# Moving the state sums and the next scores into the run of 64x64 products of a visit

## The chip, the cores and the metric

The kernel runs on one core of a Trainium2 chip. The metric is the device time of one execution, in microseconds; before the change it is 638.41 us, the median of three runs (637.95 to 638.81). The profile was taken in a further execution, whose span on the core is 636.0 us. All times below are read from that profile, in microseconds from the start of the span.

## The reference, cut to what matters

```python
# attention: 4 batches, 8 heads, 768 tokens, 64 dims
for t in range(S):
    state = gamma * state + einsum('bhd,bhe->bhde', k[:, :, t], v[:, :, t])
    y[:, :, t] = scale * einsum('bhd,bhde->bhe', q[:, :, t], state)
x = y.transpose(0, 2, 1, 3).reshape(3072, 512)
# feed-forward: 512 -> 2048 -> 512, leaky relu between
h = x @ w_in
out = maximum(0.01 * h, h) @ w_out
```

## The kernel before, in words

**Tiling.** The tokens are cut into six chunks (`c`, 0 to 5) of 128 tokens per batch. Within a chunk the recurrence is written as masked scores times values plus reads of the state; between chunks the state is a sum of keys times values. The feed-forward part works through four units (`u`, 0 to 3) of 512 hidden columns for each chunk. Its matrix products are made by a seven-product scheme at two levels, so that every unit is a chain of products on the tensor engine with additions on the vector engine and copies on the scalar engine around them. All data are FP32, and each product leaves two weight loads and two matmul records in the trace.

**Two parts.** Chunks 0 and 1 go through the feed-forward units in the first part, in which the weights are also prepared and kept in DRAM. The second part begins near 230 us. It goes through chunks 2 to 5, sixteen units (`n`), with weights that are streamed back from DRAM for each unit: `wa` for the first group of the inner products, `wb` for the second. The order of everything is written out by hand; there is no scheduler. Each engine goes through its own queue in program order, and waits on semaphores where it needs another's work.

**One unit of the second part** (main loop, L1281 to L1323) is, on the tensor engine: the inner products of the next unit with `wa` (L1184, 128x128 tiles with 128 columns), then seven output products of this unit (`output`, made by `seven`, L662, 128x128 tiles with 256 columns), with the inner products of the next unit with `wb` between the fourth and the fifth of them. The output products go in the order M1, M5, M6, M2, M7, M3, M4 into four PSUM banks named A to D, which are banks 5, 4, 7 and 6. M1 in A is copied to B by the scalar engine (L755), because M6 is added to it there. The inner products work in banks 0 to 3.

**Attention in the second part.** While chunk `c` is in units 0 and 1, the attention of chunk `c + 1` is computed, two batches at a time (a *pair*: batches 0 and 1 in unit 0, batches 2 and 3 in unit 1). There are two excursions for a pair, both with 64x64 tiles of the array, four of which work side by side:
- `scores_of_pair` (L356): the scores of the pair (L369, q against k) and the sums of keys times values for each half of the chunk (L380), 64 records each. The vector engine then masks the scores (L387, tiles `am`) and adds the sums to the state in two steps: the state in the middle of the chunk, `mid`, and the new state. It uses banks 0 to 3. It is called for the *following* pair, after the third output product. For chunk 5 the second half of the sums isn't needed, and the new state neither.
- `joint_visit` (L412): values against masked scores (L444) and reads of the old state and of `mid` with q (L427), 128 records, into banks 1, 2, 0 and 7. The vector engine multiplies the four results with the decay table `gq` and puts them into the chunk's `x` (L466, here called the *takens*). It comes right after the inner products with `wa`.

[...] So a product that follows such another waits for a mark: a GpSimd memset of one column (`rows_free`, L408), which itself waits for the last product of the earlier group. `crossed` tells which half of the rows a value product uses.

`next_gq` (L95) multiplies the decay table by one chunk's decay; it is four instructions on the scalar engine (L100), once for each new chunk, before its first pair is scored. `of_pair` loads the values (kind 1) or keys (kind 0) of a pair, `decay_v` scales the values on GpSimd, `ahead` loads q and k of a batch. `load_unit` asks for the streamed weights. All these loads are issued by one queue in program order. `outer(n + 1, 0)` (L1210) is two additions on the vector engine that follow the inner products with `wa`.

Of the kernel before, what the change touches and what calls it, by code (L numbers as in the profile page):

```python
# [22 lines left out]
def kernel(  # L23
# [329 lines left out]
    mid_of = {}  # L353
    quads = [(m, i, 2 * m + i) for m in range(HP // 2) for i in range(2)]

    def scores_of_pair(c, b, banks=None, mid=None):  # L356

        if b == 0 and c > JOINED:
            next_gq()
        banks = banks or bank  # L360
        at = [banks[j].rearrange("p (b m i t) -> p b m i t", b=2, m=HP // 2, i=2)
              for j in range(2)]
        sums = [banks[2 + h].rearrange("p (b a d) -> p b a d", b=2, a=HP) for h in range(2)]
        for n in range(2):
            x = heads[c, b + n][0]
            for m, i, a in quads:
                for h in range(2):
                    for j in range(2):
                        nc.tensor.matmul(at[j][ts(h, 64), n, m, i],  # L369
                                         lhsT=x[ts(j, 64), 1, a, ts(h, 64)],  # L370
                                         rhs=x[ts(j, 64), 0, a, ts(h, 64)],
                                         start=(n == 0 and a == 0), stop=True,
                                         skip_group_check=True)
        last = c == NC - 1
        for n in range(2):
            key, val = keys.pop((c, b + n)), vals[c, b + n]
            for a in range(HP):
                for j in range(2):
                    for h in range(1 if last else 2):
                        nc.tensor.matmul(sums[h][ts(j, 64), n, a], lhsT=key[ts(h, 64), 2 * a + j],  # L380
                                         rhs=val[ts(h, 64), 2 * a + j],
                                         start=(n == 0 and a == 0), stop=True,
                                         skip_group_check=True)
        weights = scores[c, b] = []
        for j in range(2):
            am = work.tile([128, 2, HP // 2, 2, C // 2], FP32, tag=f"am{j}", name=f"am{j}_{c}_{b}")
            nc.vector.tensor_tensor(  # L387
                out=am.rearrange("p b m i t -> p (b m i) t"),
                in0=at[j].rearrange("p b m i t -> p (b m i) t"),
                in1=mask[:, 0].unsqueeze(1).to_broadcast([128, 2 * HP, C // 2]), op=ALU.mult)  # L390
            weights.append(am)
        p = b // 2
        old = state_of[p]
        free_again[p] = [old]
        if mid is None:
            mid = halves_of_states.pop(0)
            free_again[p].append(mid)
        plus(mid, old, sums[0])
        if not last:
            state_of[p] = halves_of_states.pop(0)  # L400
            plus(state_of[p], mid, sums[1])
        mid_of[p] = old, mid
        if following(c, b) is not None and c > JOINED:
            of_pair(*following(c, b), 0)

    def rows_free(mm):

# [1 line left out]
        tc.add_manual_dep(done, mm.ins.name, IN_ORDER, reason="rows of the array")  # L409
        return done  # L410

    def joint_visit(c, b, banks=None):  # L412

        later = following(c, b) if c > JOINED else None
        banks = banks or [[bank[k] for k in at] for at in ((1, 2), (0, 7))]
        at = [[ps.rearrange("p (a t) -> p a t", t=C) for ps in of_one] for of_one in banks]
        by_half = mid_of.pop(b // 2)
        weights = scores.pop((c, b))

        def read(n, after=None):  # L420
            x = heads[c, b + n][0]
            for h in range(2):
                for m in range(HP // 2):
                    for j in range(2):
                        for i in range(2):
                            a = 2 * m + i
                            mm = nc.tensor.matmul(at[n][j][ts(i, 64), m, ts(h, 64)],  # L427
                                                  lhsT=by_half[h][ts(j, 64), n, a],
                                                  rhs=x[ts(j, 64), 0, a, ts(h, 64)],
                                                  start=(n == 0 and h == 0 and m == 0), stop=False,  # L430
                                                  skip_group_check=True)
                            if after is not None:
                                tc.add_manual_dep(mm.ins, after.name, IN_ORDER,
                                                  reason="rows of the array")
                                after = None
            return mm

        def value(n, crossed, after=None):
            val = vals[c, b + n]
            for m in range(HP // 2):  # L440
                for i in range(2):
                    for j in range(2):
                        h, a = j ^ crossed, 2 * m + i
                        mm = nc.tensor.matmul(at[n][j][ts(i, 64), m, ts(h, 64)],  # L444
                                              lhsT=val[ts(h, 64), 2 * a + j],
                                              rhs=weights[j][ts(h, 64), n, m, i],
                                              start=(n == 1 and crossed == 1 and m == 0),
                                              stop=True, skip_group_check=True)
                        if after is not None:
                            tc.add_manual_dep(mm.ins, after.name, IN_ORDER,  # L450
                                              reason="rows of the array")
                            after = None
            return mm

        done1 = rows_free(value(1, 1))
        read(0)
        done0 = rows_free(value(0, 0))
        read(1, done1)
        value(1, 0)
        value(0, 1, done0)  # L460
        for n in (1, 0):
            for j in (1, 0):
                ps = at[n][j]
                th, o = divmod((b + n) * C, N)
                blocks = xs[c][0].rearrange("p (kh th) k n -> p kh th k n", th=2)[:, :, th]
                nc.vector.tensor_tensor(out=blocks[:, j, :, ds(o, C)], in0=ps[:, 0 : HP // 2],  # L466
                                        in1=gq[:, j], op=ALU.mult)
        halves_of_states.extend(free_again.pop(b // 2))
        for n in range(2):
            heads.pop((c, b + n))  # L470
        if later is not None:
            of_pair(*later, 1)
            for n in range(2):
                decay_v(later[0], later[1] + n)

    def pair_of_banks(name):

# [2 lines left out]

    def early_scores(c, b, place):
        def do():
            banks = [pair_of_banks(f"{name}_{c}_{b}") for name in ("ap", "sp")]
            scores_of_pair(c, b, banks[0] + banks[1], place())
        return do

    def early_visit(c, b):
# [150 lines left out]

    PIECES = ((0, 0, N), (1, 0, N // 2), (1, N // 2, N))

    def seven(tiles, name, takes, takes_piece=None, order=ORDER, room=None):

        banks = {}
# [9 lines left out]
        for m, bank, sa, sb in (which[i] for i in order):  # L653
# [4 lines left out]
            for to, (i, a, z) in places:  # L658
                for n, (w, x, t) in enumerate(tiles):
                    rhs = x[:, sb] if sb < 4 else t[:, sb - 4]  # L660
                    for k in range(2):
                        nc.tensor.matmul(  # L662
                            to, lhsT=block(w, sa)[:, k, ts(i, 128)], rhs=rhs[:, k, a:z],
                            start=(first and (i == 0 or split) and n == 0 and k == 0),
                            stop=(n == len(tiles) - 1 and k == 1), skip_group_check=True)
# [385 lines left out]
    def at_of(n):  # L1051
        return 2 + n // NU, n % NU

    def load_unit(n, group):

        if n >= N2:
            return
        u = at_of(n)[1]
        if group == 0:
            wa = streamed[0]  # L1060
            nc.sync.dma_start(out=wa[:, :, 0:1], in_=kept[u][:, :, 0:1])
            nc.sync.dma_start(out=wa[:, :, 1:4], in_=kept[u][:, :, 3:6])
        else:
            wb = streamed[1]
# [194 lines left out]
    last = output(1, os[1], [parts[1]], False, True, room=room, order=FUSED)  # L1259
    products(last, 4)  # L1260
    halves_of_states.append(work.tile([128, 2, HP, D], FP32, tag="m5", name="half_states"))
    scores_of_pair(3, 0)
    for b in range(2):
        ahead(3, 2 + b)
    products(last, 1)
# [15 lines left out]
    for n in range(N2):  # L1281
# [9 lines left out]
        if n + 1 < N2:  # L1291
# [3 lines left out]
            while held:  # L1295
                held.pop()()
            products(begun, 7)
            outer(n + 1, 0)
        if visiting and u == 0:
            xs[c + 1] = new_x(c + 1)  # L1300
        if visiting:
            joint_visit(c + 1, 2 * u)
        steps = output(c, os[c], [gs.pop(n)], u == 0, u == NU - 1, room=room if more else last_room,
                       order=FUSED if more else LAST, held=held if more else None)
        products(steps, 3)
        if c + 1 < NC and u < 2 and following(c + 1, 2 * u):
            scores_of_pair(*following(c + 1, 2 * u))
        if visiting:
            load_unit(n + 2, 0)
        products(steps, 1)  # L1310
        if c + 1 < NC and u == 1:
            differences(*xs[c + 1])
        if c + 1 < NC and u == 2:
# [102 lines left out]
```

## Time and profile before

| what | value |
|---|---|
| time, median of 3 | 638.41 us |
| span of the profiled execution | 636.0 us |
| DMA, whole span | 113.42 MB, 178 GB/s |
| visits in the second part, first start | 255.69, 283.57, 357.10, 384.57, 458.29, 485.75 us |
| score runs in the second part, first start | 230.66, 263.50, 290.97, 364.50, 392.17, 465.69 us |
| granted clock of the tensor engine | 1.0 |

How to read it: "busy" of the tensor engine counts a matmul from its start to a modelled end, and matmuls overlap. An engine can therefore be busy without a gap and still work slower than it could. The distance from the start of one group to the start of the next is the better measure of what a group costs. In the timeline a line gives the start, the duration, the engine, the line of the code, the tiles of the array in use, the shape and how many records were merged; a bracket at its end gives the idle time before it and what ended it.

### The profile page before, as it was taken

To read this page: it belongs to the slowest core of one execution; us is meant where nothing else is said; L and a number is where in the kernel's file an instruction comes from. 1 tells how busy PE (TensorE), PEld (TensorE's weight loads), DVE (VectorE), ACT (ScalarE), POOL (GpSimd) and SP (SyncE) were. 2 spreads that over 40 slices of the span, in tenths; PEclk is the share of its full clock that TensorE was granted. 3 is DMA by queue.
4 is the path that set the end of the run, shared out by engine and by line. 5 is a ranking of instruction groups with operands and counts; after the bars stand their busy time and mean duration, and the time that the engine had idled before them with its cause. 6 is when DMAs were issued, how large, how long until landed. Compare 5 with 4: busy or idle time off the path is not lost.

```text
span 636.0 us, 14285 instructions
## 1 busy us (share of the span) xinstructions
PE 628.8 (99%) x6086; PEld 568.8 (89%) x6086; DVE 464.1 (73%) x760; ACT 268.9 (42%) x515; POOL 23.3 (4%) x45
## 2 busy tenths in 40 slices
PE   8999999999999999999999999999999999999997
PEld 5888888888888889899999999999999999999996
DVE  5679769889979986576785666877737768636655
ACT  4876556347343124242352442423433423534421
POOL 2000000000011010101000101000010000000000
PEclk9999999999999999999999999999999999999999
DMA  8941426556863998376735392864455236444201
GB/s 331 404 131 38 128 67 220 148 174 194 283 250 110 351 333 280 103 238 193 259 88 184 120 295 79 268 195 140 137 169 185 87 123 197 154 162 158 87 1 68
DMA packets 87537, 113.42 MB, mean 178 GB/s; under 512 B 3241, under 2 KB 71721, under 8 KB 87473
## 3 DMA queue, kind: packets, MB, share of 16 engines
q1 hardware_dynamic: 87168, 111.88, 53.2%
q8 instruction: 48, 0.79, 0.5%
q10 hardware_dynamic: 304, 0.62, 0.3%
q14 instruction: 17, 0.13, 0.1%
HBM read 93.35 MB, written 19.14 MB: 177 GB/s over the span
## 4 chain that ended last, share of the span: by engine, by line
PE 95%; DVE 2%; ACT 1%; DMA 1%; issue 0%; DVEq 0%; ACTq 0%
PE bank L662 32%; PE bank L1184 27%; PE C_h L662 4%; PE B_o L662 4%; PE A_h L662 4%; PE C_o L662 4%; PE A_o L662 4%; PE B_h L662 4%; PE D_h L662 2%; PE D_o L662 2%; PE d L683 2%; PE bank L369 1%; PE bank L444 1%; PE bank L427 1%; PE bank L380 1%; DMA t<-decay_dram 1%
## 5 line engine op out<-in xcount | busy, mean ns | idle before, releaser
L606 DVE TENSOR_TENSOR made<-made,bank 128x512 f32<-128x512 f32 (+1 forms) x96 | 56.4, 618 | 55.9 <-PE bank L1184 51.5
L606 DVE TENSOR_TENSOR o<-o,bank 128x512 f32<-128x512 f32 (+2 forms) x91 | 58.5, 661 | 51.8 <-PE bank L662 31.2
L662 PE MATMUL bank<-g,w 128*128 128x256 f32 x384 | 89.9, 382 | 0.0
L662 PEld LDWEIGHTS bank<-g,w 128*128 128x128 f32 x384 | 70.7, 190 | 9.2
L1184 PEld LDWEIGHTS bank<-x,wb 128*128 128x128 f32 x672 | 77.6, 192 | 0.8
L1184 PE MATMUL bank<-x,wb 128*128 128x128 f32 x672 | 77.6, 275 | 0.0
L1184 PE MATMUL bank<-x,wa 128*128 128x128 f32 x512 | 67.7, 275 | 0.0
L662 PE MATMUL bank<-gd,w 128*128 128x256 f32 x288 | 66.1, 379 | 0.0
L1184 PEld LDWEIGHTS bank<-x,wa 128*128 128x128 f32 x512 | 63.5, 192 | 1.1 <-ACT made L1194 0.2
L662 PEld LDWEIGHTS bank<-gd,w 128*128 128x128 f32 x288 | 54.7, 190 | 7.4
L1184 PE MATMUL bank<-t,wa 128*128 128x128 f32 x384 | 53.3, 275 | 0.0
L1226 ACT ACTIVATE g<-g 128x512 f32<-128x512 f32 x64 | 39.3, 631 | 30.8 <-DVE g L606 30.8
L1184 PEld LDWEIGHTS bank<-t,wa 128*128 128x128 f32 x384 | 48.0, 192 | 0.0
L1188 ACT COPY bank<-bank 128x512 f32<-128x512 f32 (+1 forms) x32 | 16.7, 520 | 67.8 <-PE bank L1184 67.5
L606 DVE TENSOR_TENSOR g<-made 128x512 f32<-128x512 f32 x64 | 42.7, 688 | 1.2
L755 ACT COPY bank<-bank 128x512 f32<-128x512 f32 x17 | 9.7, 570 | 71.2 <-PE bank L662 71.1
L609 DVE TENSOR_TENSOR gd<-g,gd 128x512 f32<-128x512 f32 x48 | 33.2, 692 | 5.4 <-ACT g L1226 0.5
L776 ACT COPY bank<-bank 128x512 f32<-128x512 f32 x16 | 9.1, 570 | 46.4 <-PE bank L662 46.4
L662 PE MATMUL bank<-g,last 128*128 128x256 f32 x120 | 28.3, 380 | 0.0
L662 PE MATMUL bank<-gd,last 128*128 128x256 f32 (+1 forms) x124 | 27.5, 373 | 0.0
L662 PE MATMUL A_h<-x,w 128*128 128x256 f32 x112 | 26.6, 380 | 0.0
L662 PEld LDWEIGHTS bank<-gd,last 128*128 128x128 f32 x124 | 22.8, 190 | 3.2 <-DVE gd L609 0.3
(223 smaller groups left out, 1030.1 us busy)
## 6 DMA issues: line engine op xcount, KB each, us to landing
wa<-kept SPq DMA_DIRECT2D x16, 1344.0 KB, 7.2
raw<-in_weights_dram SPq DMA_DIRECT2D x31, 512.0 KB, 4.4
wb<-kept SPq DMA_DIRECT2D x16, 896.0 KB, 5.7
wa<-kept SPq DMA_DIRECT2D x16, 448.0 KB, 4.4
wb<-kept SPq DMA_DIRECT2D x16, 448.0 KB, 6.3
out_dram<-o SPq DMA_DIRECT2D x23, 256.0 KB, 3.1
kept<-w SPq DMA_DIRECT2D x12, 448.0 KB, 6.0
qk<-in_qk_dram SPq DMA_DIRECT2D x10, 512.0 KB, 8.0
```

The source lines that it names most:

```text
L369: nc.tensor.matmul(at[j][ts(h, 64), n, m, i], lhsT=x[ts(j, 64), 1, a, ts(h, 64)], rhs=x[ts(j, 64), 0, a, ts(h, 64)], start=(n == 0 and a = ...
L380: nc.tensor.matmul(sums[h][ts(j, 64), n, a], lhsT=key[ts(h, 64), 2 * a + j], rhs=val[ts(h, 64), 2 * a + j], start=(n == 0 and a == 0), sto ...
L427: mm = nc.tensor.matmul(at[n][j][ts(i, 64), m, ts(h, 64)], lhsT=by_half[h][ts(j, 64), n, a], rhs=x[ts(j, 64), 0, a, ts(h, 64)], start=(n = ...
L606: nc.vector.tensor_tensor(out=out, in0=a, in1=b, op=ALU.add)
L609: nc.vector.tensor_tensor(out=out, in0=a, in1=b, op=ALU.subtract)
L662: nc.tensor.matmul(to, lhsT=block(w, sa)[:, k, ts(i, 128)], rhs=rhs[:, k, a:z], start=(first and (i == 0 or split) and n == 0 and k == 0), ...
L683: nc.tensor.matmul(banks[r][:, i, :], lhsT=block(2 * u, r + 2 * kh)[:, k, ts(i, 128)], rhs=x[:, 2 * kh + th, k, :], start=(step == 0 and i ...
L755: nc.scalar.copy(out=bank_of("B"), in_=ps)
L776: nc.scalar.copy(out=bank_of("D"), in_=ps)
L1184: nc.tensor.matmul(ps[q][:, i], lhsT=w[:, j, i], rhs=part_of(moving[i], s), start=(i == 0 and m in ("M1", "M5", "M4")), stop=True, skip_gr ...
L1188: nc.scalar.copy(out=ps[3], in_=ps[0])
L1226: nc.scalar.activation(g[:, i], g[:, i], AF.Prelu, alpha=0.01)
```

## The change

The two excursions of a unit become one. `scores_of_pair` is split into its parts (`scores_of`, `sums_of_states`, `masked_pair`, `new_states`), `joint_visit` into `of_visit` (which offers `read`, `value` and `taken`) and `visited`. A new `long_visit` takes the place of the visit and the score run in the main loop. It makes, in one run of 64x64 products: the crossed values, the sums of this pair's own states (into banks 5 and 4), the uncrossed values, the reads of the old state, the scores of the following pair (into banks 6 and 3), and the reads of the state in the middle. The sums so stand between the two kinds of values, which had to wait for each other's rows. A pair's state is now updated in its own visit; before, that was done with its scores, one visit earlier. The scores of chunk 3, pair 0, which have no visit ahead of them, are made alone.

Two things move with it. The additions of `outer(n + 1, 0)` come behind the visit's work on the vector engine instead of ahead of it (`behind`), and `next_gq` comes right behind them. The loads of the next weights `wa`, and then of the values and keys of the following pair, are asked for after the first output product; the weights' load carries a dependence on that product's last matmul, so that it doesn't run beside the visit. Before, the weights were asked for after the score run, the values right after the visit, and the keys of the pair after next after the score run.

The purpose is to have fewer stretches of 64x64 products between the large ones, and work between products that must wait for each other.

```diff
+    def long_visit(c, b, behind):
+        later = following(c, b)
+        read, value, taken = of_visit(c, b, [[bank[k] for k in at] for at in ((1, 2), (0, 7))])
+        done = [rows_free(value(n, 1)) for n in (1, 0)]
+        sums = sums_of_states(c, b, (bank[5], bank[4]))
+        new_states(c, b, sums)
+        for n in (1, 0):
+            value(n, 0, done[1 - n])
+        for n in (1, 0):
+            read(n, (0,))
+        if later is not None:
+            at = scores_of(*later, (bank[6], bank[3]))
+        for n in (1, 0):
+            read(n, (1,))
+        places = [(1, 1), (1, 0), (0, 0), (0, 1)]
+        if later is not None:
+            masked_pair(*later, 0, at)
+            taken(*places.pop(0))
+            masked_pair(*later, 1, at)
+        for place in places:
+            taken(*place)
+        visited(c, b)
+        behind()
+        if later is None:
+            return
+        if later[1] == 0:
+            next_gq()
+
+    def next_pair(c, b):
+        for kind in (1, 0):
+            of_pair(c, b, kind)
+        for n in range(2):
+            decay_v(c, b + n)
...
-    def load_unit(n, group):
+    def load_unit(n, group, behind=None):
...
-            nc.sync.dma_start(out=wa[:, :, 0:1], in_=kept[u][:, :, 0:1])
+            load = nc.sync.dma_start(out=wa[:, :, 0:1], in_=kept[u][:, :, 0:1])
+            if behind is not None:
+                tc.add_manual_dep(load.ins, behind.ins.name, IN_ORDER, reason="not beside the visit")
...
-    scores_of_pair(3, 0)
+    at = scores_of(3, 0, bank[0:2])
+    next_gq()
+    for j in range(2):
+        masked_pair(3, 0, j, at)
...
             products(begun, 7)
-            outer(n + 1, 0)
         if visiting and u == 0:
             xs[c + 1] = new_x(c + 1)
         if visiting:
-            joint_visit(c + 1, 2 * u)
+            long_visit(c + 1, 2 * u, lambda: outer(n + 1, 0))
+        elif more:
+            outer(n + 1, 0)
         steps = output(c, os[c], [gs.pop(n)], u == 0, u == NU - 1, room=room if more else last_room,
                        order=FUSED if more else LAST, held=held if more else None)
+        products(steps, 1)
+        if visiting:
+            load_unit(n + 2, 0, behind=newest[0])
+            if following(c + 1, 2 * u):
+                next_pair(*following(c + 1, 2 * u))
         products(steps, 3)
-        if c + 1 < NC and u < 2 and following(c + 1, 2 * u):
-            scores_of_pair(*following(c + 1, 2 * u))
-        if visiting:
-            load_unit(n + 2, 0)
-        products(steps, 1)
```

## The prediction, made before the changed kernel was run

> **What bounds the kernel now.** I read the busy times, then the chain of waits, then the tensor engine's waits in the second part (230 to 500 us), then its timeline around a visit. The first three say one thing: the chain is the tensor engine.
>
> ```profile
> PE 628.8 (99%) x6086; PEld 568.8 (89%) x6086; DVE 464.1 (73%) x760; ACT 268.9 (42%) x515; POOL 23.3 (4%) x45
> PE 95%; DVE 2%; ACT 1%; DMA 1%; issue 0%; DVEq 0%; ACTq 0%
> ```
>
> The tensor engine is busy 628.8 of 636.0 us. Among its waits between 230 and 500 us, where all that the change moves lies, there is one line:
>
> ```profile
> PE bank L427 <- DVE made L606: 0.2, 1, 0.2
> ```
>
> So taking a wait away can bring hardly anything. What is left is time in which the engine counts as busy and advances slowly, and that is seen only in the distance between starts. The timeline of the tensor engine at the visit of chunk 4, pair 0, and the run of scores and sums that follows it (start, duration, group):
>
> ```profile
> 356.34 0.83 PE L1184 MATMUL bank<-t,wa 128*128 128x128 f32 x6
> 357.10 0.46 PE L444 MATMUL bank<-am,v 64*64 64x64 f32 x16
> 357.38 0.41 PE L427 MATMUL bank<-qk,half_states 64*64 64x64 f32 x16
> ...
> 358.55 0.65 PE L444 MATMUL bank<-am,v 64*64 64x64 f32 x32
> 359.12 1.99 PE L662 MATMUL bank<-g,w 128*128 128x256 f32 x8
> 360.96 3.62 PE L662 MATMUL bank<-gd,w 128*128 128x256 f32 x16
> 364.50 1.16 PE L369 MATMUL bank<-o 64*64 64x64 f32 x64
> 365.48 1.11 PE L380 MATMUL bank<-v,k 64*64 64x64 f32 x64
> 366.53 1.99 PE L662 MATMUL bank<-g,w 128*128 128x256 f32 x8
> 368.36 4.85 PE L1184 MATMUL bank<-x,wb 128*128 128x128 f32 x42
> ```
>
> A product leaves two records. Steady steps: 80 records of 64x64 from 357.38 to 358.55, 14.6 ns each; 16 of 128x256 from 373.05 to 376.50 elsewhere in this timeline, 216 ns; 26 of 128x128 from 328.62 to 331.52, 111.5 ns. Against these the visit, 128 records, has three surcharges. The six records ahead of it last 357.10 - 356.34 = 0.76 instead of 0.67 (+0.09); the visit lasts 359.12 - 357.10 = 2.02 instead of 1.87 (+0.15, most of it in its first and last group); the eight behind it last 1.84 instead of 1.73 (+0.11). Together 0.35 us. The score run: 3.54 instead of 3.45, 2.03 instead of 1.87, 1.83 instead of 1.73, again 0.35. **An excursion into 64x64 costs about 0.35 us, however long it is.** The second part has twelve: six visits, six score runs.
>
> [...] 0.35 us at each pair of changes, and no extra step where values turn into reads at 357.38. [...] The page's instruction queue shows 48 packets for 0.79 MB, so 16 KB each[...]
>
> **The change, part by part.**
>
> Merging. The scores of the following pair and this pair's own sums move into the visit. Excursions fall from twelve to seven: six long ones, and the scores of chunk 3, pair 0, alone. The number of products is the same, and the four quarters of the array are used as before. Where chunk 5 has half the sums, 32 records take 1.03 us (393.15 to 394.18) because only two quarters work; this moves over unchanged. Saving 5 x 0.35 = 1.75 us.
>
> Order inside the run. With T its start: crossed values to T+0.52, sums to T+1.45, uncrossed values to T+1.92, old-state reads to T+2.39, next scores to T+3.32, middle-state reads to T+3.79, end E = T+3.89. Four dependences are new or moved.
> (1) The uncrossed values wait for the GpSimd marks. Marks come 0.6 to 1.1 us after the first product of their group (357.10 to 357.72; 385.32 to 386.24); now 0.93 us of sums stand between, so nothing is waited for. In the visit at 384.57 this wait is on the path today:
>
> ```profile
> 386.02 0.84 PE L444 MATMUL bank<-am,v 64*64 64x64 f32 x32
> 386.24 0.10 POOL L408 MEMSET between<- 128x1 f32 x1 [0.96 <-PE bank L444]
> 386.79 1.99 PE L662 MATMUL bank<-g,w 128*128 128x256 f32 x8
> ```
>
> The group lasts 0.77 instead of the 0.57 of the visit above: 0.20 us that go away.
> (2) The reads with the middle state wait for an addition of 0.68 us, which waits for the sums (T+1.45 and 0.23 of drain, as 365.48 to 365.71 shows before the masks) and for the vector engine, which is on the inner products' three additions until T+1.4 (356.38 + 2.11 = 358.49). Ready by T+2.4, asked for at T+3.32; even behind the second addition, T+3.1, it is early. Cost 0. Only the last visit, without scores, asks at T+2.4: 0 to 0.1.
> (3) The scores use banks 6 and 3. Bank 3 is freed by those three additions at T+1.4, asked for at T+2.39. Cost 0.
> (4) Behind the run the vector engine does mask, taken, mask, three takens (0.61 a mask from 1.29 for two, 0.33 a taken from 1.41 for four): T+3.55 to T+6.2, then two additions of the outer sums, hidden behind some 7 us of output products. The output's second product needs bank 7, free at T+4.6, asked for at E+1.84 = T+5.73. Cost 0.
>
> The one new wait on the path. After the second pair's visits of chunks 3 and 4 the scaling of the decay table (four ScalarE instructions) is now queued ahead of the copy from the first output bank to the second, on which the output's third product waits. Today the copy comes first:
>
> ```profile
> 387.40 1.41 DVE L466 TENSOR_TENSOR x<-bank,dec 128x256 f32<-128x256 f32 x4
> 388.82 0.57 ACT L755 COPY bank<-bank 128x512 f32<-128x512 f32 x1 [5.34 <-PE bank L662]
> 389.30 1.28 ACT L100 ACTIVATE dec<-dec 128x128 f32<-128x128 f32 x4
> ```
>
> The scaling waits for the takens that read the table. Third taken done at T+5.43+0.42 = T+5.85, scaling to about T+7.1 (1.28, the last overlapping), copy 0.57, third product at T+7.7. It could start at E+1.84+1.73 = T+7.46. Loss 0.24 each, 0.48 in two places; between 0 and 0.45 each, if the vector engine's steps are 0.2 faster or slower when masks and takens alternate.
>
> Start of the second part. The first score run lasts 232.82 - 230.66 = 2.16 us, 0.13 more than the others; without its sums I take the 0.13 as saved. The visit at 255.69 lasts 2.43, 0.41 too long, mostly because bank 1 is freed late (256.33). That addition follows the inner products, not what moves, so it stays.
>
> Loads. The weights for the next unit are asked for about E+2 instead of after the score run (367.08, 8 us after the visit's end), the values and keys behind them. DMA idles there and moves 300 to 400 GB/s from 366 to 381. Everything comes earlier except the value load, which has 20 us. The q and k of the following chunk, asked for at 374.3 and landing 8.2 to 9.6 us later, are now wanted at T+2.4 = 386.9 instead of 392.2; they had landed by 384.6. Cost 0 with 2.3 us in hand.
>
> Sum: -1.75 - 0.20 - 0.13 + 0.48 = -1.60, so 638.41 - 1.60 = **636.8 us**.
>
> **Rivals.**
> *Everything hides* (635.7): the scaling costs nothing, and the vector engine, free of two additions at the start, clears the waits of 0.31 and 0.36 us ahead of and in the visit at 255.69. -1.75 - 0.33 - 0.67 = -2.75. For it: the vector engine is slack. Against: those waits hang on products just before.
> *The surcharge comes back as waits* (638.0): the vector or scalar engine becomes the bound behind the run. If the third product waits 0.45 in two places and a freed bank or the middle state costs 0.1 in six visits, and the 0.33 is not found, it is -1.75 + 0.90 + 0.60 = -0.25, so 638.2; with half of those, about 637.6; I take 638.0. For it: all of the vector engine's visit work is now asked for at once. Against: the 7 us of output behind it.
> *A load comes late* (640.0, slower): the scores inside the run need q and k earlier. If they land 1.6 us late in the two visits that cross a chunk, that is +3.2 - 1.6 = +1.6. An instruction fetch that can't keep up with 512 instructions in 3.8 us would look alike. Against: 2.3 us in hand, an idle DMA[...].
>
> **How the numbers follow.** Forecast 0.55, everything hides 0.13, surcharge returns 0.20, late load 0.12. The bound of 0.2% is 1.28 us: faster means below 637.13, and the forecast with its unknowns (0 to 0.9 for the scaling) lies there four times in five. Faster 0.55 x 0.82 + 0.13 and a little of the third, 0.60; slower 0.11; same 0.29. The range runs from the second case to the upper end of the third: 635.8 to 638.4.
>
> **What would show it.** Right: one run of 256 records of about 3.9 us at each visit, no 64x64 group between output products, and surcharges of about 0.35 per run. The scaling ahead of the copy, and a third output product starting about 0.2 us late, in two visits. Wrong: a tensor-engine wait on the middle state, bank 3, or q and k; or surcharges that grow with the run's length, which would mean that they are no price of the change of mode.

## Result: 642.08 us, 0.6% slower

| | before | after |
|---|---|---|
| time, median of 4 runs | 638.18 us (637.93 to 638.81) | 642.08 us (641.45 to 642.45) |
| span of the profiled execution | 636.0 us | 640.1 us |

The ratio is 1.0059, with an interval of [1.0041, 1.0076]. A later comparison (experiment 9) gave 641.11 against 637.73, a ratio of 1.0055 [1.0041, 1.0068]. The forecast of 636.8 us was wrong in its sign.

The top of the page after the change, in the same two lines as shown of before: the busy times and the shares of the chain of waits.

```profile
PE 629.4 (98%) x6086; PEld 569.7 (89%) x6086; DVE 464.2 (73%) x760; ACT 268.9 (42%) x515; POOL 23.2 (4%) x45
PE 93%; DMA 2%; ACT 2%; DVE 2%; issue 1%; DVEq 0%
```

The busy times are those of before, the number of products is unchanged, and the granted clock is 1.0 again. New in the chain is "issue" with 1%, where it had 0%. The tensor engine's waits in the second part (from 230 us on; columns: total us, number, longest) say where it comes from:

```profile
PE bank L364 <- issue: 2.1, 2, 1.4
PE bank L433 <- issue: 1.6, 2, 1.3
PE bank L1244 <- DMA wa<-kept: 0.9, 1, 0.9
PE bank L451 <- DVE made L662: 0.2, 1, 0.2
```

Before there was one line, of 0.2 us (the last one here is a wait of 0.18 in the first visit that the kernel before has as well). L364 is the scores, L433 the reads, L451 the values: the four waits that end with "issue" lie inside the new run, and no other engine and no load ended them. In what follows v1 to v6 are the six visits of the second part in order. Here are, in the timeline, the runs of v2 (chunk 3, second pair) and of v3 (chunk 4, first pair), and the pauses in those of v4 and v5 (start, duration, group, idle time before it). v3 is the visit whose timeline the prediction shows of before.

```profile
283.20 0.69 PE L451 MATMUL bank<-am,v 64*64 64x64 f32 x32
...
285.59 1.11 PE L364 MATMUL bank<-qk 64*64 64x64 f32 x64
286.52 0.53 PE L433 MATMUL bank<-o,states 64*64 64x64 f32 x22
288.36 0.39 PE L433 MATMUL bank<-o,states 64*64 64x64 f32 x10 [1.31 <-issue]
288.68 1.99 PE L720 MATMUL bank<-g,w 128*128 128x256 f32 x8
...
360.35 0.28 PE L364 MATMUL bank<-o 64*64 64x64 f32 x5
361.99 1.09 PE L364 MATMUL bank<-o 64*64 64x64 f32 x58 [1.36 <-issue]
363.53 1.99 PE L720 MATMUL bank<-g,w 128*128 128x256 f32 x8
...
389.28 0.52 PE L433 MATMUL bank<-o,states 64*64 64x64 f32 x20 [0.27 <-issue]
...
464.87 0.34 PE L364 MATMUL bank<-o 64*64 64x64 f32 x8 [0.70 <-issue]
```

The run of v2 goes as planned, 14.6 ns a record, for 246 records; then it stops in the middle of a group of reads of which 22 have already gone out, and goes on 1.3 us later. In v3 it stops after 165 records, five records into the scores. A wait for data would be expected at the first record of a group. The bracket understates the loss, since idle time is counted from a modelled end: the whole run of v2 takes 5.48 us instead of 256 x 14.6 ns = 3.74 and the 0.15 of a visit before, so the pause cost 1.59.

**Where the 4.2 us went.** The distances between the starts of the visits place it. The first score run begins at 230.66 before and 230.57 after, so nothing came from the first part.

| stretch | before | after | difference | forecast | worked out from the trace after |
|---|---|---|---|---|---|
| first scores to v1 | 25.03 | 24.81 | -0.22 | | sums moved out -1.07, wait for `wa` +0.87 |
| v1 to v2 | 27.88 | 27.82 | -0.06 | -0.35 | excursion -0.35, slower run in v1 +0.30 |
| v2 to v3 | 73.53 | 74.76 | +1.23 | -0.11 | excursion -0.35, pause +1.59 |
| v3 to v4 | 27.47 | 28.79 | +1.32 | -0.35 | excursion -0.35, pause +1.68 |
| v4 to v5 | 73.72 | 74.05 | +0.33 | -0.31 | excursion -0.35, mark -0.20, pause +0.55, third product +0.32 |
| v5 to v6 | 27.46 | 28.04 | +0.58 | -0.35 | excursion -0.35, pause +0.92 |
| v6 to end | 150.25 | 151.26 | +1.01 | | sums moved in +1.00 |
| first scores to end | 405.34 | 409.53 | +4.19 | -1.60 | +4.21 |

The forecast for the first and last stretch together was -0.13. The pauses, 4.74 us in v2 to v5, are more than the whole loss. v1 has the same kind of loss in small: 0.19 us of its 0.30 is one step after its 146th record, in the middle of a group.

**What the pauses are.** If a run stops in the middle of a group and nothing is awaited, the instructions themselves may be missing. Three readings point to it. First, the DMA view of the stretch from 284 to 292 us (40 slices of 0.2 us, busy tenths and GB/s) shows the pause with nearly idle DMA engines, and two packets of the instruction queue around it:

```profile
DMA  0000000040000000000000000002000000000000
GB/s 0 0 0 0 0 0 0 0 82 0 0 0 0 0 0 0 0 0 0 0 0 0 0 0 0 0 0 82 0 0 0 0 0 0 0 0 0 0 0 0
...
q8 instruction: 2, 0.03, 1.8%
```

One packet begins at 285.7; the engine stops at 287.05 and goes on at 288.36, 2.7 us after that packet began, and the next packet begins at 289.5, 1.1 us after the engine has gone on. The other pauses have the same order: in v3 to v5 the engine goes on 2.9, 2.4 and 2.7 us after a packet began, and the next one begins 1.0 to 1.1 us later.

Second, the page shows 48 packets of the instruction queue (`q8 instruction`) for 0.79 MB, 16 KB each. The tensor engine has 6086 matmul records, 127 to a packet, and in experiment 2 six packets come with 768 records, 128 each. So I take a packet to hold a block of 128 records (an estimate from these counts), or 256 instructions, since the page counts a weight load beside each matmul record (x6086 both); the 6086 records make 47.5 such blocks. Between the four pauses the trace has 637, 382 and 765 records; 5, 3 and 6 blocks are 640, 384 and 768 (the two or three records less are not accounted for).

Third, all four pauses come at the second block's edge in a run, if the edges lie 128 records apart (at 118 and 246 in v2, 37 and 165 in v3, 9 and 137 in v4, 56 and 184 in v5). The runs of 128 records before the change cross one edge each, or none, and had no pause.

### The profile page after: what moved, and what is told of

It is laid out like the page before. It is cut to its first block, busy times and chain, and to the rows that moved or that the text cites. A ratio compares the mean times of both kernels' runs of the same rounds, so it can differ in the third digit from the quotient of the medians.

```text
span 640.1 us, 14280 instructions
## 1 busy us (share of the span) xinstructions
PE 629.4 (98%) x6086; PEld 569.7 (89%) x6086; DVE 464.2 (73%) x760; ACT 268.9 (42%) x515; POOL 23.2 (4%) x45
## 4 chain that ended last, share of the span: by engine, by line
PE 93%; DMA 2%; ACT 2%; DVE 2%; issue 1%; DVEq 0%
PE bank L720 31%; PE bank L1244 26%; PE C_h L720 4%; PE B_o L720 4%; PE A_h L720 4%; PE C_o L720 4%; PE A_o L720 4%; PE B_h L720 4%; PE D_o L720 2%; PE D_h L720 2%; PE d L741 2%; DMA wa<-kept 1%; PE bank L451 1%; PE bank L364 1%; PE bank L433 1%
```

## Experiments

The fetch theory is that a dense run uses instructions faster than they come: 128 records in 1.87 us, where the next block takes some 3.5 us (an estimate from v2: these 1.87 and the 1.59 lost there). Its rivals are that some product or operand inside the run is slow, that the loads or the vector engine's later work disturb it, and that the loss is the price of a longer run in itself. In the expectations FETCH stands for the first, and WAIT for a semaphore or a change of the kind of product as the cause; pairs are named there by their first batch, so that v2 is "chunk 3, pair 2"; "the mixed version" is the kernel of experiment 6, and "the plain split" that of experiment 5.

**1. The same program, shifted by 26 records.** If block edges cause the pauses, products added far ahead must move them by just so many records. Ten idle products at the start of the kernel become 36 shorter ones; these are not FP32 and leave one record each (in the changed kernel the ten, and one more behind them, leave 11).

```diff
+    def small_ones(count, cols):
...
-    keep_busy(10)
+    small_ones(36, 128)
```

> The changed kernel with 26 more weight-load and matmul pairs (52 instructions) ahead of everything on the tensor engine: the ten idle products of 512 columns at the start become 36 of 128 columns. Nothing else moves. In the changed kernel the run of products pauses after record 246 of the visit of chunk 3, pair 2 (1.31 us), after record 165 of chunk 4, pair 0 (1.36 us), after record 137 of chunk 4, pair 2 (0.27 us). Theory FETCH [...]: every pause comes 26 records earlier, after 220 and 139; the third visit, whose block edge falls out of the run's start, pauses instead near record 239 and for about 1.3 us, while the pause after 139 shrinks to about 0.3 us[...]. Time 641 to 643. Theory WAIT (the pauses belong to a semaphore or to a change from one kind of products to another): the pauses stay after records 246, 165 and 137, with their lengths.

Measured: 644.10 us against 637.66, ratio 1.0087 [1.0061, 1.0113]. That is above the 641 to 643 expected, but the 2.2 us by which the profile's span is longer lie ahead of the second part (its first scores start at 232.88). There the granted clock is 0.5 from 13.7 to 17.1 us (0.997 in the mean of the execution), where the changed kernel has 1.0; the one run of the four with a mean clock of 0.999 took 641.4 us, the others, at 0.994 to 0.997, 644 and more. From the first scores to the end it takes 409.42 us, where the changed kernel takes 409.53. The timeline of the runs of v2 and v4:

```profile
288.91 1.10 PE L364 MATMUL bank<-qk 64*64 64x64 f32 x60
290.88 0.27 PE L364 MATMUL bank<-qk 64*64 64x64 f32 x2 [0.87 <-issue]
...
392.00 0.41 PE L433 MATMUL bank<-o,half_states 64*64 64x64 f32 x15
393.44 0.47 PE L433 MATMUL bank<-o,half_states 64*64 64x64 f32 x17 [1.02 <-issue]
```

In v2 the pause comes after 160 + 60 = 220 records, where it came after 246: moved by exactly 26, and now between two scores. In v4 the edge of 137 moved to 111, and the pause came at the one after it, 239. In v5 it moved from 184 to 158, and 0.44 us are left. The pause in v3, whose edges moved to 11 and 139, is gone, and v1 got one of 1.36 us after 248 and one of 0.34 after 120, the only one at a run's first edge (by the same count the edge before it lies eight records ahead of the run). No product is slow by nature; what counts is where in the instruction stream the run lies. Shifting the program only moves the loss from run to run.

**2. A much longer run.** 384 products of 64x64 on constants, with results that nothing reads, are added between two large stretches near 408 us: 768 records with no operand to wait for.

```diff
+    def long_run():
+        for _ in range(6):
+            for m in range(16):
+                for i in range(2):
+                    for j in range(2):
+                        nc.tensor.matmul(bank[2 * j][ts(i, 64), 0:64],
+                                         lhsT=mask[ts(j, 64), 0], rhs=mask[ts(j, 64), 0],
+                                         start=True, stop=True, skip_group_check=True)
...
+        if n == 6:
+            long_run()
```

> The changed kernel with 384 more 64x64 products (768 records, 1536 instructions) of constant operands into two free banks, in one run ahead of the inner products of the seventh unit, near 431 us; nothing waits for their results. At 14.6 ns a record they need 11.2 us. FETCH [...]: after the first 128 to 256 records a pause about every 128 records, one block each 3.5 us, 17 to 20 us for the run. [...] WAIT: no pause either, since nothing in the run waits.

Measured: 662.45 us, in one run. The timeline of the tensor engine, and the DMA view of 407 to 429 us (busy tenths in slices of 0.55 us):

```profile
407.74 2.67 PE L1348 MATMUL bank<-mask 64*64 64x64 f32 x167
413.31 5.55 PE L1348 MATMUL bank<-mask 64*64 64x64 f32 x256 [2.90 <-issue]
420.49 2.09 PE L1348 MATMUL bank<-mask 64*64 64x64 f32 x128 [1.64 <-issue]
423.95 2.09 PE L1348 MATMUL bank<-mask 64*64 64x64 f32 x128 [1.36 <-issue]
427.40 1.55 PE L1348 MATMUL bank<-mask 64*64 64x64 f32 x89 [1.36 <-issue]
```

```profile
DMA  9999999100000100000100000010000010000001
```

This isolates the cause. With nothing to wait for, the run settles at 128 records every 3.46 us (420.49 to 423.95, 423.95 to 427.40), 27 ns a record instead of 14.6. The DMA engines do nothing in these stretches but carry one block every 3.5 us (30 GB/s in one slice of six or seven, 0 in the others): what limits is the time until a block comes, not their bandwidth. The same view counts `q8 instruction: 6`, six packets for the 768 records. The first pause, after 167 records, is longer, 2.90 us. Until about 411 us the DMA engines are full of data, and the packet it waits for begins only at 410.8. The 256 records behind it last 5.55 us for a second reason: from 413.3 to 416.4 the granted clock is 0.5 (0.997 in the mean of the execution), and a record takes 26.7 ns. From 416.4 on it is 1.0 again, so also in the blocks on which the 3.46 us rest. In all the run lasts 21.2 us; 17 to 20 were expected.

**3. Loads asked for beside the run.** The change asks for the weights only behind the run's first output product. This kernel asks at its start.

```diff
         if visiting:
+            load_unit(n + 2, 0)
             long_visit(c + 1, 2 * u, lambda: outer(n + 1, 0))
...
-            load_unit(n + 2, 0, behind=newest[0])
```

> The changed kernel with the streamed weights asked for at the start of the run instead of behind the first output product: 1.8 MB are then moved beside the run. FETCH: the blocks of instructions come over the same DMA engines; in the long run of constant operands a block that was asked for while data were moved held the engine up for 2.90 us instead of 1.36. So the pauses get 1 to 2 us longer in the five long visits that have one, and shift to no other record: 646 to 652 us. WAIT: nothing in the run uses these weights, so the pauses stay as they are, and the time stays at 642.

Measured: 656.55 us in one run, more than any theory had it. The run of v2 in the timeline, to be read against the one of the changed kernel above:

```profile
287.12 0.53 PE L433 MATMUL bank<-o,states 64*64 64x64 f32 x22
292.26 0.39 PE L433 MATMUL bank<-o,states 64*64 64x64 f32 x10 [4.60 <-issue]
```

The pause is at the same record, 246, and lasts 4.60 us instead of 1.31: data keep the DMA engines full from 285.5 to 292.4, where they were nearly idle in the changed kernel, and the engine goes on at 292.26. The DMA view of 284 to 294 us has two instruction packets among 2111 of data:

```profile
q1 hardware_dynamic: 2111, 2.88, 81.9%
q8 instruction: 2, 0.03, 1.4%
```

In v3 the pause is again at 165, and lasts 2.57; in v5 it lasts 3.08, and one of 2.35 comes behind the run of v4, where the next block ends. So the blocks share the DMA engines with the data and are late among them: 4.60 us of pause against 1.31 at the same record. The waits with "issue" add up to 13.6 us instead of 3.7. The expectation missed the rest: behind three of these pauses (4.60, 2.35 and 3.08) the granted clock is 0.5 for 3.4 us (0.992 in the mean of the execution), and an output record takes 427 ns instead of 216. At half speed that is an estimated 1.7 us each, 5 us in all; with the 9.9 us of waits it makes about the 14.5 us by which this time exceeds the changed kernel's. The part of the change that moves the loads behind the run is therefore right in itself, and worth some 14 us in this comparison.

**4. The sums of chunk 3, pair 0, back with its scores.** This shortens v1 to 192 records, and gives the tensor engine back the microsecond after which it met the load of `wa` near 249 us.

```diff
-        sums = sums_of_states(c, b, (bank[5], bank[4]))
-        new_states(c, b, sums)
+        if (c, b) != (3, 0):
+            sums = sums_of_states(c, b, (bank[5], bank[4]))
+            new_states(c, b, sums)
...
     at = scores_of(3, 0, bank[0:2])
+    sums = sums_of_states(3, 0, bank[2:4])
...
+    new_states(3, 0, sums)
```

> The changed kernel with the state sums and the new state of chunk 3, pair 0, made with its scores, as before the change; the first visit's run has 192 records instead of 256. In the changed kernel the inner products wait 0.87 us for the streamed weights at 249.15, which the kernel before does not. FETCH and the reading that the start is bound by that load: the wait at the load goes (-0.9), and the first visit is shorter by its 64 records without giving them back, and has no pause: about 640.9 us. If the load's wait comes from the changed order of the loads instead, the wait stays, and the time stays at 642 within 0.3.

Measured: 640.88 us, ratio 1.0053 [1.0031, 1.0074]; from the first scores to the end 408.95 us in place of 409.53. There is no wait for `wa` and no pause in v1, and those of v2 to v5 stay (0.97, 1.03, 0.79, 0.61). The time is as expected. (The profile is of a run of 643.89 us, with the granted clock at 0.5 from 7.8 to 11.2 us, far ahead of the second part; so the distance is the better measure.) But the wait for `wa` is also absent in experiments 1, 2 and 5, and shorter in experiment 3 (0.29) and when the changed kernel ran again (0.42), although these don't move the sums. So it varies between executions, and how much of it belongs to the change isn't settled.

**5. A first cure: the run cut in two.** The first output product (`between` is `products(steps, 1)`) goes between the reads of the old state and the next scores, so that no stretch has more than 160 records.

```diff
         for n in (1, 0):
             read(n, (0,))
+        if between is not None:
+            between()
         if later is not None:
             at = scores_of(*later, (bank[6], bank[3]))
```

> The changed kernel with the first output product (8 records of 216 ns in 128x128 tiles) put into the run, between the reads of the old state and the next scores, in the five visits that have scores: runs of 160 and 96 records instead of 256. FETCH: while the slow product runs the next block arrives; pauses of more than 0.3 us stay only where a block edge is left within the first 160 records. It adds five excursions of 0.35 us (1.75) and takes away the pauses (the runs are 5.0 us too long in the four visits from the second to the fifth, of which 0.15 each is the surcharge) and 0.3 us of the third output product's wait, because the copy is now queued ahead of the table's scaling: 642.1 - 4.7 - 0.3 + 1.75 = 638.8 us. WAIT, with the pauses due to what the scores or the middle-state reads wait for: the product takes the place of the pause, and 1.7 us of it are hidden, so about the same. WAIT, with the pauses due to the change of kind inside 64x64 products: the pauses stay, 643.5.

Measured: 645.96 us, ratio 1.0125 [1.0107, 1.0142]: missed by 7 us. The pauses did go (one of 0.42 is left, in v1), and other waits came. The two largest of the tensor engine's waits:

```profile
PE bank L722 <- DVE x L466: 3.3, 5, 0.7
PE bank L1246 <- ACT bank L1250: 1.2, 1, 1.2
```

The first is bank 7: the output's second product follows the run's end directly, with no first product between, and the vector engine hasn't yet taken the read out of that bank. The prediction's "free at T+4.6, asked for at E+1.84" held only because of the 1.84 us of the first product. The second comes from GpSimd: in the timeline the scaling of the values now stands beside two additions of the vector engine.

```profile
275.71 2.49 POOL L161 TENSOR_TENSOR v<-v,dec 128x512 f32<-128x512 f32 x2 [19.48 <-DMA v<-in_kv_dram]
```

```profile
275.84 1.46 DVE L664 TENSOR_TENSOR g<-made 128x512 f32<-128x512 f32 x1
277.23 1.53 DVE L664 TENSOR_TENSOR g<-g,made 128x512 f32<-128x512 f32 x1
```

The addition that follows takes 0.68 us again; these two take 1.46 and 1.53 while GpSimd works, and GpSimd's two operations take 2.49 us together instead of 2.04. So the additions about double and GpSimd's work takes a fifth more while they overlap; why isn't shown.

**6. A cure for those waits.** Experiments 4 and 5 together (v1, with 192 records, isn't cut), the output in the order M1, M6, M5, so that bank 7 is wanted one product later, and the values and keys asked for in mid-run, ahead of the weights, so that GpSimd is done earlier.

```diff
+    SPLIT = (0, 1, 2, 4, 5, 6, 3)
...
         if visiting:
-            load_unit(n + 2, 0, behind=newest[0])
             if following(c + 1, 2 * u):
                 next_pair(*following(c + 1, 2 * u))
+            load_unit(n + 2, 0, behind=newest[0])
```

> Built from the above: sums of chunk 3, pair 0, early (first visit in one run of 192 records); in the visits of chunk 3, pair 2, to chunk 5, pair 0, the first output product inside the run; behind the run the third output product (into bank 4) ahead of the second (into bank 7), so that it doesn't meet the 0.66 us wait for bank 7 that the plain split ran into; values and keys asked for ahead of the weights, so that GpSimd doesn't scale the values while the vector engine makes the outer sums (there these took 1.46 instead of 0.69 us each, and the tensor engine waited 1.16 us). FETCH: no pause above 0.3 us, eleven excursions instead of twelve, the wait for the GpSimd mark gone: 0.4 to 0.8 us below the kernel before, about 637.5. WAIT with the scores or middle reads as its cause: 639 or more, with the wait turning up elsewhere.

Measured: 640.78 us, ratio 1.0038 [1.0025, 1.0052], where about 637.5 was expected: missed. Both waits of experiment 5 are gone, but this one came, behind the run of v4, with two shorter pauses, 0.27 us in v3 and 0.17 in v4. Here is the group in the timeline, and the DMA view of 386 to 393 us (slices of 0.175 us):

```profile
392.74 3.61 PE L724 MATMUL bank<-gd,w 128*128 128x256 f32 x16 [1.86 <-issue]
```

```profile
DMA  0010004945547999999999995300000000000000
```

The values and keys keep the DMA engines full until 390.2 us, and the block of instructions comes through only at their end. It is experiment 3 in small, made by my own edit.

**7. The first visit cut as well.**

```diff
-        split = visiting and following(c + 1, 2 * u) and n > 0
+        split = visiting and following(c + 1, 2 * u)
```

> The same with the first visit split as well: one more excursion, so 0.35 us longer in the distance from the first scores of the second part to the end (both theories), with no pause in the first visit either way; in the time, 0 to 0.6 us longer.

Measured: 640.59 us, ratio 1.0040 [1.0028, 1.0053], no difference to experiment 6 that the times tell. What it was made for is in the trace: v1 to v2 takes 27.25 us with two excursions and 26.89 with one. An excursion costs 0.36 us, as the prediction had it. The whole distance from the first scores to the end was expected to grow by as much and did not (407.99 against 407.94), because v3 to v4 is 0.42 shorter here; the pause of 0.27 in v3 isn't in this execution.

**8. The loads kept off the cut run too.** Experiment 6, with the values and keys carrying the dependence on the output product behind the run, as the weights do.

```diff
-    def next_pair(c, b):
+    def next_pair(c, b, behind=None):
...
-                next_pair(*following(c + 1, 2 * u))
+                next_pair(*following(c + 1, 2 * u), behind=newest[0])
```

> The last mixed version with its loads behind the run again: the values and keys of the following pair carry the same dependence on the output product behind the run as the weights, and are asked for ahead of them. In the mixed version they were asked for in the middle of the run, and in the visit of chunk 4, pair 2, a block of instructions came only after them: a pause of 1.86 us behind the run. FETCH: that pause goes, no other above 0.3 us comes, and the distance from the first scores of the second part to the end is 2 to 2.5 us shorter than in the mixed version (407.9 there, 405.3 in the kernel before): 637.6 to 638.4, level with the kernel before or up to 0.4 us faster, since eleven excursions stand against twelve. WAIT: the pause stays.

Measured: 638.94 us against 637.73 (14 and 18 runs), ratio 1.0018 [1.0010, 1.0026], so still slower than before, and 0.5 above the range expected; the distance is 2.1 us shorter than in experiment 6, as expected. From the first scores to the end it takes 405.81 us, against 405.34 before and 409.53 after the change (408.82 when the changed kernel ran again, on the chip of this experiment). This is the whole list of the tensor engine's waits in its second part:

```profile
PE bank L453 <- DVE made L667: 0.2, 1, 0.2
```

It is the list of before again. So with the run cut and data kept off it the pauses are gone. Of the second part's 3.5 us, 3.0 come back (408.82 - 405.81, of 408.82 - 405.34; single traces, that of before from the first comparison). In the medians it is 2.2 of 3.4 us (641.11 - 638.94, of 641.11 - 637.73). A gain isn't left. Eleven excursions should be 0.35 better than twelve, but v1 gives that back: without sums between its two kinds of values, 48 records take 1.05 us instead of 0.70, because they wait for the marks (the GpSimd memsets of `rows_free`, for which a value product waits that uses the other half of the rows than those before it). A little of the lateness is also left: the output product inside the run takes 0.23 us more in v3 than in v2, and in v4 the 32 reads at 385.61 take 0.93 us to the next start, where the same group takes 0.58 in v2. In the trace both losses begin with one late record, after 164 records in v3 and after 136 in v4, within one record of where the changed kernel paused (165 and 137). No version tried beats the kernel before.

**9. The changed kernel again**, in the same comparison as experiment 8.

> The changed kernel itself, unaltered, on the chip of the last version, as a measure for it. FETCH and WAIT: 641 to 643. The 0.87 us wait of the inner products for the streamed weights near 249 us, which its first profile shows and those of the lengthened start, the split and the long run of constant operands do not, is either here again, or was a matter of that execution's transfers.

Measured: 641.11 us, as given above. The pauses are again after 246, 165 and 137 records (1.02, 1.08 and 0.17 us), with 0.65 in v5, and here v1's loss after 146 records counts as one too (0.42). Their places are those of the program. In v2 and v3 the first trace had some 0.3 us more (1.31 and 1.36); why isn't known.

## Why the prediction was wrong

**Right.** The price of an excursion is 0.35 us (experiment 7: 0.36), and five of them were saved; every stretch of the table closes with that figure to 0.02. The wait for the GpSimd mark at v4 is gone. The middle state, bank 3, and q and k cost nothing: in v4 the middle state is made at 388.44 + 0.69 = 389.13, which is T + 2.38 (forecast T + 2.4), and the first read of it goes out at 390.52. The weights come in time in all units but the first.

**Right in kind, off in size.** The scaling ahead of the copy was put at 0.24 us in two places; it cost 0.32 in one. In the timeline after v4 the copy stands behind the scaling, and the third output product waits for it:

```profile
393.02 3.94 PE L720 MATMUL bank<-gd,w 128*128 128x256 f32 x16
393.15 1.28 ACT L100 ACTIVATE dec<-dec 128x128 f32<-128x128 f32 x4 [7.49 <-DVE x L466]
394.34 0.57 ACT L813 COPY bank<-bank 128x512 f32<-128x512 f32 x1
...
396.79 1.89 PE L720 MATMUL bank<-g,w 128*128 128x256 f32 x8
```

The second and third product together last 396.79 - 393.02 = 3.77 us instead of 3.45. After v2 they last 3.45: the pause comes late in that run, and the vector engine catches up while the tensor engine stands still; there the scaling begins 0.5 us after the run's end, in v4 2.0.

**The step that failed** is "An excursion into 64x64 costs about 0.35 us, however long it is". It was drawn from runs of 128 records only, one block of instructions, and carried over to 256. The missing term is the pause at the second block's edge: 1.59 + 1.68 + 0.55 + 0.92 us, and some 0.3 in v1. The prediction named costs that grow with the run's length as a sign of being wrong; this is what came. The prediction also had the cause in view: its third rival says that "an instruction fetch that can't keep up" would look like a late load. That enough instructions would be at hand ahead of a run was the author's estimate; no trace of before shows it, and here it is contradicted: v3 stops after 330 instructions, although some 70 us of large products lie between it and v2, in which by an estimate 20 blocks could come at one every 3.46 us. Experiment 2 stops after 334.

**How the pause's length follows**, now that the runs show the numbers. By an estimate from experiment 2 (3.46 us from block to block) a block comes about 3.5 us after the engine goes over to the block before it. A dense run uses a block in 1.87 us (128 x 14.6 ns). So at the second edge in a run 3.5 - 1.87 = 1.6 us are missing, which is what v2 and v3 lost. In v4 the first edge lies nine records into the run, and the packet begins 0.15 us after the run does (386.90 and 386.75). If it is asked for 1.1 us ahead, as the packets behind the pauses suggest, it was asked for before the run began, while a record still took 111.5 ns, and only 0.55 is missing. In v5 the sums take twice as long, 0.47 us more; by this sum 1.1 should be missing, and 0.92 is. That a block is asked for when an edge is crossed is inferred from these lengths and from the packets' starts; no record shows the asking.

**The start** was mis-sized too. The sums that left the first score run shortened it by 1.07 us, as they should; the tensor engine then came to the inner products near 249 us before their weights had arrived, in this execution. The prediction looked at the loads around the visits, and not at the one after the first score run.

## What to carry to other kernels

Count instructions, not only time, when short products are merged: here the pauses inside the visits came at a run's second block edge, 137 to 248 records (274 to 496 instructions) into it, but for one of 0.34 us at a first edge (experiment 1), and the blocks of a long run came 3.46 us apart (experiment 2). Runs of 128 records, one block, had no pause; runs of 256, which always hold two edges, lost up to 1.7 us. Cut into 160 and 96 records by one long product, with no transfer beside them, they lost at most 0.36. Where a limit lies between these was not measured. In a profile this stall is an idle time ended by "issue" in the middle of a group of like instructions; shift the program by some instructions, and if the pause moves by just as many, it is the fetch.

## What was not expected of the hardware

- In the long run of experiment 2 the tensor engine got 256 instructions every 3.46 us, with idle DMA engines: 74 instructions per us, where 64x64 FP32 products take 137.
- Data transfers delay instruction blocks: pauses of 4.60 instead of 1.31 us (experiment 3), 1.86 (experiment 6) and 2.90 (experiment 2). In experiments 2 and 6 the instruction packet began only at the end of the transfer (at 410.8 and 390.4), and the engine went on 2.5 and 2.4 us after it began.
- A pause can cost twice. Behind four of the five pauses over 2 us (2.90 in experiment 2; 4.60, 2.35 and 3.08, but not 2.57, in experiment 3) the granted clock of the tensor engine was 0.5 for 3.1 to 3.4 us.
- Additions of the vector engine take 1.46 and 1.53 us instead of 0.68 beside GpSimd's (experiment 5).

**Open.** Why the wait for `wa` near 249 us is there in some executions, why the pauses are longer in some, and why the clock falls behind some long pauses and not behind all. That the program could be laid out so that no run holds two block edges in a bad place wasn't tried; with 256 records in a run there are always two.
